# Output scatters without an order among themselves, each behind a one-element write on GpSimd

## The chip, the cores and the metric

The kernel runs on one core of one Trainium2 chip. The metric is device time in microseconds (us), the median of several runs. The engines are named as the profile names them: PE (TensorE matmuls) and PEld (its weight loads), DVE (VectorE), ACT (ScalarE), POOL (GpSimd), SP (SyncE, which only issues transfers here).

## The reference

Causal attention is followed by a mixture of experts with a capacity, and that by a dense layer pair. Cut to what matters:

```python
attn_out = attention(q, k, v, s)              # (4, 8, 576, 64), float32
x = attn_out.transpose(0, 2, 1, 3).reshape(2304, 512)
# every token goes to one of 8 experts, at most 288 tokens each, best logits first
for e in range(8):
    mask = assigned == e                       # 288 tokens
    h = np.maximum(x[mask] @ w1[e], 0.0)       # (288, 512) @ (512, 1024)
    out[mask] = h @ w2[e]
h = out @ w_in                                 # (2304, 512) @ (512, 2048)
g = np.maximum(h, 0.0) + alpha * np.minimum(h, 0.0)
return g @ w_out                               # (2304, 512)
```

The expert of a token decides the order in which the kernel works on it, and each of the 2304 output rows belongs to exactly one expert's list of 288.

## The kernel before

Attention comes first (until about 285 us of the profiled span) and leaves its result token by token in a tensor in device memory, `xd`. Then the experts are taken one after another, in the order in which a router (class `Router`) finds them. For each expert n the kernel does four things. It gathers the 288 token rows from `xd` in three blocks of 96 rows, through tiles called `stg` (`gather`, L775, an indirect DMA that GpSimd issues). It runs the expert's own two layers (`L1` and `L2` with `kind` 0). It runs the dense pair (`L1` and `L2` with `kind` 1). Last, it takes the result `oT`, which lies with features on partitions, back to token rows and scatters them to the output `out_dram`.

Every product is made of three matmuls of split operands, a high part and a low part. GpSimd makes the low parts of many of them: of the weights, `w0r` and `w1r` (L654, in `split`), and of the activations between the dense layers, `hh` (L746). So GpSimd's queue holds these subtractions and, in a fixed place among them, the gathers and scatters.

The order is written out by hand: the program's order is each engine's order, and `hook()` is called between the pieces of the matmul stream to emit the next pieces of the side tasks (`prep`, `routing`, `outs`). The scatters are such side pieces. There are 24 of them, three for each of eight experts:

- For the first seven experts `ot_dma` is used. For block j it packs 96 token columns as two-byte halves (`A`, L823 and L824), transposes them by a DMA from ScalarE's queue (`T`), puts the halves together into a `stg` tile on VectorE (`Y`, L830) and scatters that tile (`Z`, L831). `stg` has two buffers, which the gathers share: the third block of an expert uses the first block's buffer again, and the two gathers that follow use the second's and the third's. `relay` spreads the steps over the ticks; a split of a weight lies between one scatter and the next on GpSimd.
- For the eighth expert `ot` is used, at the very end: a transpose on PE, a copy on ScalarE (L787) and the scatter (L788), three times. The third block has a tile of another ring (`a64`), so none of the three waits for a buffer of the others.

A framework places the waits. It knows the scatters only as writes to the tensor `out_dram` at rows that it can't see, so each scatter waits until the one before has landed.

Of the kernel before, what the change touches and what calls it, by code (L numbers as in the profile page):

```python
# [12 lines left out]
F = dt.float32  # L13
# [24 lines left out]
TP1=0  # L38
# shifts of events against their tick and their place in it
SH={"T_peq": -0.2, "load_qk1q0": -1.58, "lg_pe": 1.83, "v3_act0_0": 0.33, "lt_act": 0.1, "load_v15": -0.27, "v2_pool": 0.06, "load_v12": 0.14, "v1_act0_0": -1.29, "spin": 0.17, "load_v11": 0.75, "T_pek": -0.1, "finish_tail": -0.2, "T_dveq": -0.13, "T_dvek_0": -0.17, "T_pek_0": -0.74, "load_qk1q2": -1.13, "v1_act1_0": -0.36, "mins20": 0.07, "T_actk_0": 0.07, "rd_4": 2.79, "lg_dve": 1.56, "load_bias": 0.68, "load_qk1q3": -0.45, "load_qk1q1": -1.43, "v2_dve_0": -0.2, "lt_pe": 1.31, "load_v14": 1.48, "load_qk1q4": -0.5, "load_qk1k1": -0.26, "v3_act1": -0.94, "T_peq_0": -4.8, "rd_1": -0.73, "load_qk1k3": -0.09, "mins00": 0.07, "tail_act": -0.1, "T_dveq_0": -0.69, "load_qk1k2": 0.42, "rd_2": -0.13, "tail_pe_0": -1.05, "tail_dve_0": -0.27, "v3_act0": 0.03, "v1_pool": 0.13, "etr2": 0.79, "v1_act0": 0.76, "rd_3": 1.2, "mins30": -0.26, "finish": 0.07, "lt_dve": 0.94, "v1_act3_0": -0.1, "av1": 1.9, "v3_dve1_0": -0.13, "v2_pool_0": 0.13, "lt_T": -0.2, "av2": 0.43, "load_v10": -0.06, "load_qk1k0": -0.32, "tail_act_0": -0.93, "v1_pool_0": -0.13, "v1_act1": 0.24, "T_actk": -0.12, "etr0": 0.23, "T_actq": 0.06, "norm_main": 0.37, "v3_dve0": 1.63, "v3_dve1": 0.11, "mins31": -0.14, "T_dvek": -0.17, "av0": 1.59, "v1_act2_0": -0.51, "etr3": 0.23, "split_lo0": 0.07, "split_lo1": 0.6, "split_hi2": -0.23, "split_lo2": -0.13, "split_hi3": 0.63, "split_lo3": 0.77}  # L40
V1N=4
ORDER=('pe0','pe1','pe2','pe3','dve0','dveA','dveB','act1','sp','dve2','act2','dve3','pl','act3','ld')
def attention(tc, q, k, v, s, w_gate, xd, L, C, cp, ap, psum, dp, hook=None, rawp=None):
    rawp=rawp or ap
    nc=tc.nc
    B,NH,S,D=4,8,576,64
    NP=B*NH//2
    idf,idb,ones=C['idf'],C['idb'],C['ones']
    # ---- loads
    warmt=ap.tile([128,8],F,name='warmt')  # L50
# [24 lines left out]
    for nm in 'qk': load_qk1(0,nm,4)  # L75
    # ---- masks
    SB=[ap.tile([128,2304],R,name=f'sb{i}') for i in range(2)]
# [5 lines left out]
    nc.vector.tensor_copy(mkt[0:64,:],mk[0:64,0:64]); nc.vector.tensor_copy(mkt[64:128,:],mk[64:128,64:128])  # L83
    # ---- keeps the array's clock up until the products begin
    def spin(n):
        tp=psum.tile([128,512],F,name='tp',bufs=TPB)
        for _ in range(n): nc.tensor.matmul(tp[:,0:128],mk,mk,start=True,stop=True)
    spin(SP0)
    # ---- cumulative sums
    nc.vector.tensor_scalar(st,st,0.0,None,op0=OP.max)  # L90
# [38 lines left out]
    for pp in range(2):  # L129
        for ab in range(2):  # L130
            # rows (pp,d) of block j: pair 2j+pp, head 2*pair+ab
            src=w_gate.rearrange("(j pp ab d) e -> pp ab d j e",j=2,pp=2,ab=2,d=64)
            nc.sync.dma_start(wgt[pp*64:pp*64+64,:,ab,:], src[pp,ab])
    ZT=ap.tile([128,2,2,128],F,name='zt'); nc.gpsimd.memset(ZT,0.0)
    # ---- q, k transposes and splits
    OPS={}
# [76 lines left out]
    def v3_dve(hb,z):  # L213
# [3 lines left out]
        nc.vector.scalar_tensor_tensor(vhl[:,1],vr,c,vhl[:,0],op0=OP.mult,op1=OP.subtract)  # L217
    # ---- scores and softmax
    SM={}; DEN={}
    # steps of a head pair: q tiles (0, 1), 2, 3 and the 64-row tail of both heads  # L220
    PARTS={0:((0,0),(1,128)),1:((2,0),),2:((3,0),)}
    WID={0:384,1:384,2:512}
    def qk(p,i):
# [3 lines left out]
        if i<3:  # L227
            qh,ql=OPS['q',p]
            # the two heads' products lie on different rows of the array and run side by side
            for ti,off in PARTS[i]:  # L230
# [163 lines left out]
    def lt_dve(b):  # L394
        r=slice(64*(b%2),64*(b%2)+64)
        nc.vector.tensor_copy(L[r,16+b//2,:],LG.pop(('l',b,4))[r,0:8])
    # ---- pipeline
    steps=[(p,i) for p in range(NP) for i in range(4)]
    n=len(steps)
# [61 lines left out]
    for t in range(tmin,tmax+1):  # L461
        while ev and ev[0][0]<t+1:
            _,f,a=ev.pop(0); f(*a)
# [3 lines left out]
NT,NE,CAP=18,8,288  # L467
# [27 lines left out]
class Router:  # L495
# [11 lines left out]
    def big(self): return self.rp.tile([128,NT*((1<<max(BS))-1)],BF,name='A')  # L507
    # The threshold t: the largest value that some open expert has CAP tokens at or above,
    # and the first such expert. Thresholds are float bits in value order, found from the top bits down.
    def search(self,mm,idx,ts,es,k):  # L510
# [5 lines left out]
        for s in range(32-B,-B,-B):  # L516
# [23 lines left out]
            if top:  # L540
                V.tensor_reduce(dig,ps[:,0:8],axis=AX.X,op=OP.max)
                # key to bits: flip the sign bit of the upper half, every bit of the lower half
                f=rp.tile([128,2],I,name='wsg')
# [18 lines left out]
    def phase(self,k,out):  # L562
# [11 lines left out]
        yield YE  # L574
        if k==NE-1: es=idx[:,0:1]; nw=NT   # one expert is left, for all the tokens left
        else:
            ts=rp.tile([128,1],F,name='ts'); es=rp.tile([128,1],F,name='es'); nw=2*NT
            for y in self.search(mm,idx,ts,es,k): yield y
# [13 lines left out]
        nc.tensor.matmul(p2[:,0:nw],self.tri,Gf,start=True,stop=True)  # L592
        # places: of the tokens above the threshold, then of those at it; 1023 and more for the others
        sc=rp.tile([128,nw],F,name='sc'); s18=rp.tile([128,NT],I,name='s18')
# [25 lines left out]
        out['idx']=idt  # L620
        # state for the next phase
        if k<NE-1:
# [11 lines left out]
class FFN:  # L634
# [11 lines left out]
    def start(self,router,xd,w1,w2,out,fp,psum):  # L646
        nc=self.nc; self.r=router; self.xd=xd; self.w1=w1; self.w2=w2; self.out=out
        self.fp=self.fpa=fp; self.psum=psum; self.idf=router.idf
        self.xT=[fp.tile([128,4,CAP],R,name=f'xT{z}') for z in 'hl']
        for c in range(self.nl,2*ND-NLOAD): self.load64(c)  # L650
    # ---- resident weights
    def split(self,h,l,x,lo_eng):
        self.nc.scalar.activation(h,x,AF.Copy)  # L653
        lo_eng.tensor_sub(l,x,h.bitcast(F))  # L654
    # float64 bits -> float32: sign and top exponent bit, seven exponent bits and 23 of the significand's.
    # Chunk 2f: w_in's columns of f-tile f; chunk 2f+1: w_out's rows. The split weights take the bits' place.
    # Where chunk c lies: a ring of its own, a slot that attention has done with, or a ring of the FFN's pool.
    def slot64(self,c,shape,dtype):
# [39 lines left out]
    def early_conv(self,n):  # L698
        for _ in range(n):
            if self.nc64<self.nl: self.cstep(1)  # L700
    # ---- expert weights
    def reg(self,n,ei):
# [10 lines left out]
    def wsplit(self,n,i):  # L713
# [4 lines left out]
        self.W[n,f,which]=w  # L718
    # ---- layers
    def L1(self,n,kind,f):  # L720
# [27 lines left out]
    def L2(self,n,kind,f):  # L748
# [12 lines left out]
        if f==last:  # L761
# [3 lines left out]
            for d in range(4):  # L765
# [4 lines left out]
                else: nc.scalar.activation(self.oT[:,d],a,AF.Copy)  # L770
    # ---- token-major ends
    def mi(self): return self.r.mi()
# [10 lines left out]
    def ot(self,idt,j,eng=None):  # L783
        nc=self.nc; ps=self.mi(); s=slice(96*j,96*j+96)
        for d in range(4): nc.tensor.transpose(ps[0:96,128*d:128*d+128],self.oT[:,d,s],self.idf)
        t=(self.fp.tile([128,512],I,name='a64',bufs=PB).bitcast(F) if j==2 else self.fp.tile([128,DM],F,name='stg',bufs=2))[0:96]
        nc.scalar.activation(t,ps[0:96,:],AF.Copy)  # L787
        nc.gpsimd.indirect_dma_start(out=self.out,out_offset=bass.IndirectOffsetOnAxis(ap=idt[:,j:j+1],axis=0),in_=t,in_offset=None)  # L788
    # the same by DMA: the transpose takes two-byte elements, so the floats go as planes of halves
    def planes(self): return self.fp.tile([128,512],I,name='a64',bufs=PB).bitcast(U16)  # L790
# [28 lines left out]
    def ot_dma(self,oT,idt):  # L819
        nc=self.nc; V=nc.vector; a={}; b={}; t={}  # L820
        def A(j):
            a[j]=self.planes(); av=a[j].rearrange("p (z d n) -> p z d n",z=2,d=4)
            V.memset(av[:,:,:,96:128],0)  # L823
            V.tensor_copy(av[:,:,:,0:96],oT.bitcast(U16)[:,:,192*j:192*j+192].rearrange("p d (n z) -> p z d n",z=2))  # L824
        def T(j):
            b[j]=self.planes()
            self.flip(b[j],a[j])
        def Y(j):
            t[j]=self.fp.tile([128,DM],F,name='stg',bufs=2)[0:96]
            V.tensor_copy(t[j].bitcast(U16).rearrange("p (e z) -> p z e",z=2),b[j][0:96].rearrange("p (z e) -> p z e",z=2))  # L830
        def Z(j): nc.gpsimd.indirect_dma_start(out=self.out,out_offset=bass.IndirectOffsetOnAxis(ap=idt[:,j:j+1],axis=0),in_=t[j],in_offset=None)  # L831
        return self.relay(A,T,Y,Z,OW)
    # ---- schedule
    def hook(self):
# [13 lines left out]
    def prep(self,n,o):  # L848
        yield lambda: self.l2done>=n   # the expert before has read its tokens and its weights
        self.reg(n,o['e'])  # L850
# [30 lines left out]
    def run(self):  # L881
# [15 lines left out]
        self.cstep(NX)  # L897
        # keeps the array's clock up while the tokens arrive
        def spin(n):
# [158 lines left out]
```

## Time and profile before

| | |
|---|---|
| median of three runs | 1031.24 us |
| the three runs | 1024.48, 1031.24, 1032.9 us |
| span of the profiled execution, first to last instruction | 1021.2 us |
| the profiled execution's own time | not given; the median lies 10.0 us above the span |
| PE busy | 913.3 us, 89% of the span |
| VectorE busy | 647.7 us, 63% |
| GpSimd busy | 501.1 us, 49% |
| ScalarE busy | 456.9 us, 45% |
| the last instruction of PE's products starts at | about 1008 us |

The span is that of one execution, taken by the hardware profiler. All rows further on are of that execution, in us from the start of the span. Issuing a transfer, a wait on a semaphore and a drain are work of an engine's queue and are not counted as busy, except that GpSimd's indirect DMAs are shown as instructions of POOL: their duration is the time in which GpSimd makes the transfer, not the transfer itself.

### The profile page before, as it was taken

What the parts mean: (1) busy time and instruction counts of PE and PEld (TensorE: products, weight loads), DVE (VectorE), ACT (ScalarE), POOL (GpSimd) and SP (SyncE); (2) the same over time, 40 slices, a digit from 0 to 9 for tenths busy, and PEclk for the clock granted to TensorE, in tenths of its full rate; (3) what the DMA queues carried; (4) which work ended last, traced back from release to release, by engine and by line L of the source; (5) the groups of instructions that cost most, each with busy time, mean ns of one, the idle gap of its engine ahead of it and who ended that gap; (6) DMA issues with size and microseconds to landing.
All of it is one profiled execution on the core that took longest, in us unless ns stands there. A gap on an engine that the chain in (4) does not pass through costs nothing.

```text
span 1021.2 us, 21290 instructions
## 1 busy us (share of the span) xinstructions
PE 913.3 (89%) x8043; PEld 844.5 (83%) x8043; DVE 647.7 (63%) x1413; ACT 456.9 (45%) x1234; POOL 501.1 (49%) x460
## 2 busy tenths in 40 slices
PE   6898999884438898999999999999999999999995
PEld 5677777763427788999999999999999999999994
DVE  7888888898885987856676545645654533332310
ACT  4677777753213334433334344334434444444332
POOL 6555655556244457725255355526526526535322
PEclk9899999986558999999999999999999999999998
DMA  6999999987765021313263035207205313422200
GB/s 124 210 240 212 212 223 211 260 182 130 237 224 180 16 64 52 98 36 98 61 158 84 17 73 143 52 22 173 67 8 137 102 29 88 127 53 73 45 1 24
DMA packets 269878, 116.10 MB, mean 114 GB/s; under 512 B 207504, under 2 KB 257040, under 8 KB 269776
## 3 DMA queue, kind: packets, MB, share of 16 engines
q1 hardware_dynamic: 127728, 70.56, 25.9%
q10 hardware_dynamic: 138976, 34.75, 20.0%
q0 software_dynamic: 3072, 9.44, 3.1%
q8 instruction: 63, 1.03, 0.4%
q14 instruction: 39, 0.32, 0.1%
HBM read 70.39 MB, written 9.58 MB: 78 GB/s over the span
## 4 chain that ended last, share of the span: by engine, by line
PE 49%; DVE 14%; DMA 6%; issue 6%; POOL 4%; ACT 2%; SPq 1%; POOLq 0%; DVEq 0%; ACTq 0%
PE hp L728 8%; PE acc L758 8%; PE hp L729 8%; PE hp L730 7%; PE acc L760 7%; PE acc L759 7%; DMA out_dram<-stg,idt 3%; PE mi L533 2%; DVE g L740 1%; POOL hh L746 1%; DMA et<-eh 1%; DVE a L680 1%; DVE a L682 1%; DVE a L681 1%; DMA rB<-in_moe_w_out_dram 1%
## 5 line engine op out<-in xcount | busy, mean ns | idle before, releaser
L746 POOL TENSOR_TENSOR hh<-g,hh 128x288 fp32r<-128x288 f32 x128 | 118.3, 925 | 246.3 <-ACT hh L745 214.9
L740 DVE SCALAR_TENSOR_TENSOR g<-g,nal 128x288 f32<-128x288 f32 x128 | 76.6, 599 | 162.2 <-ACT g L739 150.5
L294 POOL TENSOR_TENSOR eh<-e,eh 128x768 f16<-128x768 f32 (+1 forms) x48 | 91.1, 1899 | 69.7 <-DVE eh L283 43.3
L654 POOL TENSOR_TENSOR w0r<-wraw,w0r 128x512 fp32r<-128x512 f32 x62 | 89.6, 1445 | 58.2 <-ACT w0r L653 58.0
L738 ACT ACTIVATE g<-hp 128x288 f32<-128x288 f32 x128 | 52.3, 409 | 135.9 <-PE hp L730 121.8
L745 ACT ACTIVATE hh<-g 128x288 fp32r<-128x288 f32 x128 | 56.9, 444 | 117.9 <-DVE g L740 117.9
L758 PE MATMUL acc<-hh,rB 128*128 128x288 f32 x352 | 106.2, 302 | 0.0
L760 PE MATMUL acc<-hh,rB 128*128 128x288 f32 x352 | 104.3, 296 | 0.0
L759 PE MATMUL acc<-hh,rB 128*128 128x288 f32 x352 | 104.1, 296 | 0.0
L728 PE MATMUL hp<-x2h,rB 128*128 128x288 f32 x320 | 90.8, 305 | 0.0
L729 PE MATMUL hp<-x2h,rB 128*128 128x288 f32 x320 | 89.7, 300 | 0.5 <-POOL rB L654 0.5
L734 DVE SCALAR_TENSOR_TENSOR hh<-hp,hh 128x288 fp32r<-128x288 f32 x64 | 29.0, 453 | 84.7 <-ACT hh L733 84.7
L271 ACT ACTIVATE e<-sc,mn 128x128 f32<-128x128 f32 (+3 forms) x128 | 66.2, 528 | 34.5 <-DVE mn L261 24.7
L759 PE MATMUL acc<-hh,w1r 128*128 128x288 f32 x256 | 76.5, 299 | 0.9 <-POOL w1r L654 0.9
L758 PE MATMUL acc<-hh,w1r 128*128 128x288 f32 x256 | 77.1, 301 | 0.0
L760 PE MATMUL acc<-hh,w1r 128*128 128x288 f32 x256 | 76.1, 297 | 0.0
L728 PE MATMUL hp<-xTh,w0r 128*128 128x288 f32 x256 | 73.9, 308 | 0.9 <-ACT xTh L781 0.6
L729 PE MATMUL hp<-xTh,w0r 128*128 128x288 f32 x256 | 73.2, 305 | 0.3 <-POOL w0r L654 0.3
L758 PEld LDWEIGHTS acc<-hh,rB 128*128 128x128 f32 x352 | 66.5, 189 | 0.3
L760 PEld LDWEIGHTS acc<-hh,rB 128*128 128x128 f32 x352 | 66.5, 189 | 0.0
L654 POOL TENSOR_TENSOR w1r<-wraw,w1r 128x512 fp32r<-128x512 f32 x46 | 64.1, 1393 | 4.8 <-ACT w1r L653 4.6
L759 PEld LDWEIGHTS acc<-hh,rB 128*128 128x128 f32 x352 | 66.3, 188 | 0.0
(297 smaller groups left out, 2907.6 us busy)
## 6 DMA issues: line engine op xcount, KB each, us to landing
wraw<-in_moe_w_dram SPq DMA_DIRECT2D x128, 256.0 KB
rB<-in_moe_w_out_dram SPq DMA_DIRECT2D x11, 512.0 KB
rB<-in_moe_w_in_dram SPq DMA_DIRECT2D x10, 512.0 KB
qr<-in_q_dram SPq DMA_DIRECT2D x32, 128.0 KB
kr<-in_k_dram SPq DMA_DIRECT2D x32, 128.0 KB
vr<-in_v_dram SPq DMA_DIRECT2D x32, 128.0 KB
xd<-xm SPq DMA_DIRECT2D x16, 256.0 KB
rA<-in_moe_w_in_dram SPq DMA_DIRECT2D x3, 512.0 KB
```

What stands on the lines that cost most here:

```text
L271: nc.scalar.activation(e[:,h,off:off+N],sc[:,off:off+N],AF.Exp,bias=mn[:,2*z+h:2*z+h+1],scale=-1.0,accum_out=den[:,2*ti+h:2*ti+h+1])
L294: nc.gpsimd.tensor_sub(e4[:,:,1],e[:,:,:N],e4[:,:,0])
L654: lo_eng.tensor_sub(l,x,h.bitcast(F))
L728: nc.tensor.matmul(ps,wh[k],x[0][:,k],start=(k==0),stop=False)
L729: nc.tensor.matmul(ps,wl[k],x[0][:,k],start=False,stop=False)
L730: for k in range(4): nc.tensor.matmul(ps,wh[k],x[1][:,k],start=False,stop=(k==3))
L740: nc.vector.scalar_tensor_tensor(g,g2[:,1],self.nal[:,f:f+1],g,op0=OP.mult,op1=OP.add)
L745: nc.scalar.activation(hh[:,0],g,AF.Copy)
L746: nc.gpsimd.tensor_sub(hh[:,1],g,hh[:,0].bitcast(F))
L758: nc.tensor.matmul(a,wh[:,ds],hh[:,0],start=(f==0),stop=False)
L759: nc.tensor.matmul(a,wl[:,ds],hh[:,0],start=False,stop=False)
L760: nc.tensor.matmul(a,wh[:,ds],hh[:,1],start=False,stop=(f==last))
```

## The change

The two places that issue a scatter call a new function. It writes one element of a new tile `mark` on GpSimd and then issues the scatter, which is put into a group whose members are declared to have no dependence on each other. Waits of a scatter for its data, and of others for a scatter, are not touched by the declaration. Nothing reads `mark`. (The diff also takes out comments.)

```diff
@@ start
         self.xT=[fp.tile([128,4,CAP],R,name=f'xT{z}') for z in 'hl']
+        self.mark=fp.tile([1,1],F,name='mark')
@@ ot
-        nc.gpsimd.indirect_dma_start(out=self.out,out_offset=bass.IndirectOffsetOnAxis(ap=idt[:,j:j+1],axis=0),in_=t,in_offset=None)
+        self.scatter(idt,j,t)
+
+    def scatter(self,idt,j,t):
+        self.nc.gpsimd.memset(self.mark,0.0)
+        i=self.nc.gpsimd.indirect_dma_start(out=self.out,out_offset=bass.IndirectOffsetOnAxis(ap=idt[:,j:j+1],axis=0),in_=t,in_offset=None)
+        self.tc.declare_no_dep(i.ins,group='out',reason='rows of different tokens')
+        self.tc.add_to_no_dep_group('out',i.ins)
@@ ot_dma
-        def Z(j): nc.gpsimd.indirect_dma_start(out=self.out,out_offset=bass.IndirectOffsetOnAxis(ap=idt[:,j:j+1],axis=0),in_=t[j],in_offset=None)
+        def Z(j): self.scatter(idt,j,t[j])
```

## Rows read from the trace of the kernel before

**Rows 1.** The page's head, and busy time in two stretches of the span.
```profile
span 1021.2 us, 21290 instructions
...
600.00:700.00 100.00, 98.51 (x810) 95.54 (x809) 51.95 (x123) 41.30 (x96) 53.09 (x45) 1.00 0.37 85
...
1000.00:1021.00 21.00, 8.53 (x63) 7.70 (x61) 0.69 (x2) 4.88 (x11) 4.37 (x5) 0.79 0.10 28
```

**Rows 2.** PE's waits from 320 us to the end: total us, times, longest.
```profile
PE mi L613 <- DVE rb L609: 5.7, 4, 2.0
...
PE acc L760 <- POOL hh L746: 2.2, 2, 1.2
...
PE acc L759 <- POOL w1r L654: 0.9, 3, 0.5
```

**Rows 3.** GpSimd's instructions by line: count, busy us, mean ns, idle before.
```profile
L831 POOL DMA_INDIRECT out_dram<-stg,idt x21 | 20.3, 965 | 36.9 <-DMA out_dram<-stg,idt 19.7 <-DVE stg L830 4.3 <-DVE hh L734 4.0
```

**Rows 4.** GpSimd's timeline around the third expert's scatters: start, us, idle before.
```profile
612.06 0.94 POOL L831 DMA_INDIRECT out_dram<-stg,idt  x1 [0.15 <-issue]
...
616.87 0.93 POOL L831 DMA_INDIRECT out_dram<-stg,idt  x1 [2.54 <-DMA out_dram<-stg,idt]
617.82 1.29 POOL L654 TENSOR_TENSOR w1r<-wraw,w1r 128x512 fp32r<-128x512 f32 x1
621.83 0.92 POOL L831 DMA_INDIRECT out_dram<-stg,idt  x1 [2.71 <-DMA out_dram<-stg,idt]
...
625.74 1.95 POOL L775 DMA_INDIRECT stg<-xd,idt  x1 [1.74 <-PE hp L730]
627.72 1.55 POOL L746 TENSOR_TENSOR hh<-g,hh 128x288 fp32r<-128x288 f32 x2
```

**Rows 5.** VectorE's timeline in the same stretch.
```profile
614.80 0.75 DVE L830 COPY stg<-a 96x1024 uint16<-96x1024 uint16 x1
...
619.07 0.76 DVE L830 COPY stg<-a 96x1024 uint16<-96x1024 uint16 x1 [0.86 <-DMA a<-a]
```

**Rows 6.** The timeline of the last 13 us, ScalarE's last copy and GpSimd.
```profile
1008.44 0.92 POOL L788 DMA_INDIRECT out_dram<-stg,idt  x1 [3.69 <-ACT stg L787]
1008.90 0.59 ACT L787 ACTIVATE a<-mi 96x512 f32<-96x512 f32 x1 [0.25 <-PE mi L785]
1011.98 0.92 POOL L788 DMA_INDIRECT out_dram<-stg,idt  x1 [2.62 <-DMA out_dram<-stg,idt]
1015.51 0.92 POOL L788 DMA_INDIRECT out_dram<-a,idt  x1 [2.61 <-DMA out_dram<-stg,idt]
```

**Rows 7.** The chain that ended last, its last stretch: start, us, what.
```profile
1008.44 2.76 DMA out_dram<-stg,idt
...
1011.24 0.74 issue
```

**Rows 8.** GpSimd's timeline, first gathers after attention: indirect DMAs issued back to back.
```profile
299.07 1.15 POOL L775 DMA_INDIRECT stg<-xd,idt  x1 [3.12 <-DVE acc L624]
300.52 1.36 POOL L775 DMA_INDIRECT stg<-xd,idt  x1 [0.31 <-issue]
```

**Rows 9.** Small writes of GpSimd at the start of the program, by line.
```profile
L1040 POOL MEMSET const-float32-1.0<- 128x1 f32 x1 | 0.1, 107 | 0.0
```

**Rows 10.** The program's last line: GpSimd's drains, ns min/median/max, first and last start.
```profile
L1054 POOLq DRAIN  x3: 40/102/5133, 1015.3 to 1021.0; - x3
```

**Rows 11.** Busy time in 1008.4 to 1012.0 us; DMA share and GB/s last.
```profile
1008.40:1012.00 3.60, 0.46 (x4) 0.21 (x2) 0.00 (x0) 0.84 (x2) 0.94 (x2) 1.00 0.20 57
```

**Rows 12.** A scatter of the first expert and VectorE's copy beside it.
```profile
431.60 1.30 POOL L831 DMA_INDIRECT out_dram<-stg,idt  x1 [0.16 <-issue]
...
431.59 0.49 DVE L824 COPY a<-x2h 128x768 uint16<-128x768 uint16 x1
```

**Rows 13.** Busy time in 523 to 528 us; granted clock third from the end.
```profile
523.00:528.00 5.00, 4.76 (x38) 4.73 (x38) 4.73 (x15) 0.63 (x1) 2.49 (x2) 0.66 0.54 147
```

**Rows 14.** Time from issue to landing of the first three gathers, 295 to 330 us.
```profile
DMA to landing us min/median/max: 3.7/6.8/8.3
```

## The prediction

> **What bounds the kernel now.** I read the page's head first, then busy time by stretches. From about 500 us on the kernel is a stream of matmuls: between 600 and 700 us PE is busy 98.5 of 100 us at a granted clock of 1.00, GpSimd 53 [rows 1]. Nothing that GpSimd does can count there unless PE waits for it. The last 21 us are different: PE is busy 8.5 of them [rows 1], its work is over at about 1008 us, and what follows is a chain with one step at a time.
>
> Next I read who PE waits for from 320 us on. Two groups name GpSimd: 2.2 us in two waits for `hh`, 0.9 us in three waits for `w1r`, together 3.1 us [rows 2]. The dearest single cause is another: 5.7 us in four waits of the router's product for `rb` on VectorE, the longest 2.0 us [rows 2].
>
> Then I read the scatters. 21 of the 24 have line 831; GpSimd sat idle 36.9 us before them, 19.7 of it until an earlier scatter had landed [rows 3]. The other three stand at the end of the program, and there the wait before the second and the third is 2.62 and 2.61 us [rows 6]. So the order among scatters costs GpSimd some 25 us of idle time. The question is how much of it lies on the path that sets the end.
>
> **The change part by part.** *The last three scatters.* They start at 1008.44, 1011.98 and 1015.51 us, 3.54 and 3.53 us apart [rows 6]. Such a step is the landing, 2.76 us from the issue, and 0.74 us more until the next one is under way [rows 7], with a few hundredths for the wait. Their data are no obstacle: the third block's copy starts at 1008.90 and takes 0.59 us, so it is done at 1009.49, and the second block's was done before it [rows 6]. Without the order, a step is what GpSimd itself needs: 0.92 us for the scatter [rows 6], about 0.10 for the small write (107 ns for a 128x1 write [rows 9]; no 1x1 write is in the trace, and a smaller one is hardly dearer), and the gap in front of an indirect DMA behind another, 0.31 us [rows 8]. That is 1.33 us. The third scatter then starts at 1008.44 + 2.66 = 1011.10 in place of 1015.51: 4.4 us earlier. The first write costs nothing, since GpSimd idles 3.69 us before the first scatter [rows 6]. Bounds on the step: 0.92 + 0.15 = 1.07 us, if only the short gap of a scatter behind a subtraction applies [rows 4] and the write hides in it, and 1.36 + 0.31 + 0.10 = 1.77 us by the slower of the two gathers [rows 8]. The gain lies between 3.5 and 4.9 us.
>
> What comes after the last scatter could eat this. GpSimd's final drain takes 5.13 us from 1015.3 [rows 10], so it ends at 1020.4, while the scatter that it follows should have landed at 1015.51 + 2.76 = 1018.3: 2.2 us more. With one scatter open the surplus is 2.2 us; with three open the trace has no row. If each open scatter added such a surplus in turn, 4.4 us would be added and the gain would be nil; it may as well not grow at all. I take no growth, because the drain starts with a single scatter in flight in the only row there is and I see nothing that would make it go by scatters. So the tail is worth 4.4 us, with ends 0 and 4.9.
>
> *The transfers in the tail.* The DMA engines are busy 0.20 of the 3.6 us around the first scatter [rows 11], 0.7 us of all sixteen for one scatter. That is below the step of 1.33 us, so one is through before the next arrives, and I keep the landing time at 2.76 us. The far end is the three gathers issued back to back, which took 3.7 to 8.3 us to land [rows 14], but beside heavy loads that the tail doesn't have.
>
> *The 21 scatters in the middle.* Take the third expert's [rows 4]. The second scatter waits 2.54 us for the first; its data, a copy that starts at 614.80 and takes 0.75 us, are there at 615.55 [rows 5], so it can go at about 615.75, 1.1 us earlier than 616.87. The split of `w1r` behind it moves with it, and PE's wait for that goes. The third scatter's data come at 619.07 + 0.76 = 619.83 [rows 5], so it goes at about 620.05 in place of 621.83, 1.8 us earlier; from here the data, not the order, are late. Behind it stand two gathers that write into `stg` buffers still being read by the second and third scatter. They keep their waits: the wait moves from the third scatter to the first gather, and the second gather still waits for the third scatter's landing. That landing is 1.8 us earlier, so `hh`, at 627.72 now, comes up to 1.8 us earlier. This is one of the two `hh` waits of 1.0 and 1.2 us (2.2 in all), and both should go. The other stands behind the sixth expert's scatters, and the three `w1r` waits behind the third, the sixth and the seventh expert's. Behind the other four groups PE names nothing of GpSimd, so an earlier start is worth nothing there. I take the whole 3.1 us of [rows 2] as the gain; the bounds are 0 (VectorE becomes late in the same places) and 3.1 plus one vanished router stall.
>
> *The small write.* 21 x 0.1 us = 2.1 us of GpSimd time in the middle. It waits for nothing, so it runs at once behind the instruction ahead of it, where GpSimd sits idle for want of data or room. If that cover is gone in all 24 places, it costs 2.4 us.
>
> *A rule against it.* A scatter that starts beside VectorE's copy at 431.59 took 1.30 us in place of 0.93 or so [rows 4, 12], 0.37 us more. The Trainium skill, page "SBUF — State Buffer", section "SBUF: two separate sides", warns that GpSimd cannot write a DMA's descriptors while VectorE runs a two-port operation such as a float32 copy. The trace agrees in kind, 1.30 against 0.93 us. By the rule each moved scatter could be held for the length of such a copy, and the sum of the middle would be smaller; by the row it keeps its gain. Here the moved scatters follow the copy that makes their data, by about 0.2 us, and at most 0.37 us of the 1.1 to 1.8 would be lost. In the tail VectorE does nothing [rows 11].
>
> Sum: 4.4 + 3.1 = 7.5 us. The profiled execution's own time isn't given; its span, 1021.2 us [rows 1], lies 10.0 us below the median of 1031.24, and nothing of the change touches what lies outside. So the span should be 1013.7 us and the median 1031.24 - 7.5 = 1023.7 us.
>
> **Rivals.** *Tail only: 1026.8 us.* The PE waits in the middle are replaced by others: `hh` also needs ScalarE's and VectorE's work, and a gather behind the third scatter keeps its wait for the landing. For it: the wait moves rather than goes. Against: PE's named waits there end on GpSimd. 1031.24 - 4.4 = 1026.8.
>
> *More than counted: 1020.0 us.* GpSimd's earlier work clears VectorE's router chain of one stall. Each has a price: 2.0 us of wait [rows 2], and in the 5 us after such a stall the granted clock averaged 0.66 [rows 13], a part of it at 1.2 in place of 2.4 GHz, which is 5 x 0.34 = 1.7 us: 3.7 in all. One stall less gives 1020.0, two 1016.3.
>
> *Open scatters get in each other's way: 1029.7 us.* If a scatter doesn't move before the earlier one has landed, only the 0.74 us and the wait itself, 0.78 us, are saved twice, and the middle gains nothing: 1031.24 - 1.6. Against it is the low DMA share.
>
> *The change doesn't do what it says: 1031 to 1034 us.* If the waits stay, for the buffers or for a reason of the framework's, the 24 writes are all that is new, from 0 to 2.4 us. Against: in the tail the three tiles are different, so only the order can hold them.
>
> *Slower: 1038.5 us.* GpSimd's subtractions move by 1 to 2 us against VectorE's router chain, and where they now fall beside its long operations both take longer (a gather took 1.95 us at 625.74, against 0.92 for the scatters [rows 4]). If the router's product becomes late by a stall of 3.7 us in a further phase, half the gain is gone; from the third such phase on (3 x 3.7 = 11.1 against 7.5) the kernel is slower, and with four it is at 1031.24 - 7.5 + 14.8 = 1038.5. Over 1% slower takes five of the six phases behind a group. Against: the chain has few such stalls now, four in 700 us.
>
> **How the numbers follow.** Chances: forecast 0.42, tail only 0.27, more than counted 0.13, scatters in each other's way 0.05, no effect 0.07, slower 0.06. The range reaches from 1018, which takes in the case of one stall less and part of that of two, to 1031, which takes in the 1029.7 and the drain's bound without the middle; beyond it lie slower, most of no effect and part of the low case, about 2 in 10. A measurement of this kernel can tell about 1% from no change, 10.3 us: the three runs alone span 8.4 us. 1% faster is below 1020.9. That holds most of the case of one stall less or more, and some of the forecast's own spread by the runs: 0.25. Slower by over 1%, above 1041.6, takes the slower case at its worst: 0.04. The rest is 0.71.
>
> **What would show it.** Right: the last three scatters some 1.3 us apart with no wait between them, the span's end some 5.7 us behind the third as now (1021.2 - 1015.51), no wait of a line-831 scatter for `out_dram`, gathers that now carry the wait for a landing, and no `hh` or `w1r` wait of PE around 615 to 630, 865 to 885 and 945 to 955 us. Wrong: a drain well above 5.1 us, a landing well above 2.8 us in the tail, or new waits of PE for the router's VectorE steps. What would make the number wrong with every step right is a shift of the whole stream in its first 400 us, where no scatter stands.

## The result, and the profile after

| | before | after |
|---|---|---|
| median, first comparison (4 runs each) | 1032.07 us | 1018.58 us |
| ratio, first comparison | | 0.9882, 95% interval 0.9836 to 0.9927 |
| ratio, second comparison (9 runs against 28) | | 0.9908, 95% interval 0.9873 to 0.9943 |
| span of the profiled execution | 1021.2 us | 1017.2 us |
| that execution's own time | | 1019.14 us |

The change makes the kernel faster, by about 1%. (A ratio is estimated from all runs of its comparison and isn't the quotient of the two medians.) The two ratios make 12.2 us (7.5 to 16.9) of 1032.07 and 9.5 us (5.9 to 13.1) of 1028.62. The spans differ by 4.0 us only. The reason is that the profiled execution of before had a short attention stage: its first gather starts at 299.07 us [rows 8], that of after at 305.79. The next section shows how far such starts scatter.

The end of the kernel first. GpSimd's timeline over the last 10 us, after; it answers to [rows 6] and [rows 9]:

```profile
1009.01 0.92 POOL L793 DMA_INDIRECT out_dram<-stg,idt  x1 [3.66 <-ACT stg L788]
1009.93 0.09 POOL L792 MEMSET mark<- 1x1 f32 x1
1010.24 0.92 POOL L793 DMA_INDIRECT out_dram<-stg,idt  x1 [0.22 <-ACT a L788]
1011.16 0.09 POOL L792 MEMSET mark<- 1x1 f32 x1
1011.46 0.92 POOL L793 DMA_INDIRECT out_dram<-a,idt  x1 [0.22 <-issue]
```

The scatters are 1.23 us apart where they were 3.54: 0.92 for the scatter, 0.09 for the write, 0.22 until the next is under way. The third starts 2.45 us behind the first, before 7.07.

The program's last line after, GpSimd's drains (ns min/median/max, first and last start); it answers to [rows 10]:

```profile
L1061 POOLq DRAIN  x3: 40/102/6272, 1010.1 to 1016.9; - x3
```

The long drain is 1.14 us longer than before, but it also starts earlier against the last scatter: just ahead of the second scatter (1010.1 against 1010.24), where before it started just ahead of the third (1015.3 against 1015.51). It ends at 1016.4, 4.9 us after the start of the third scatter, as before (1020.4 against 1015.51). The end of the span is 5.71 us behind the start of the last scatter in both executions, so the drain doesn't grow with three scatters open. Nor does the landing: in a second execution of the changed kernel (`both_again` below) each of the last three scatters took 2.7 us from issue to landing, against 2.7 to 2.8 us before.

The middle, by the third expert's scatters again. GpSimd's timeline after; it answers to [rows 4]:

```profile
618.74 0.94 POOL L793 DMA_INDIRECT out_dram<-stg,idt  x1 [0.16 <-issue]
...
622.52 0.93 POOL L793 DMA_INDIRECT out_dram<-stg,idt  x1 [1.49 <-DVE stg L837]
623.47 1.30 POOL L655 TENSOR_TENSOR w1r<-wraw,w1r 128x512 fp32r<-128x512 f32 x1
624.70 0.09 POOL L792 MEMSET mark<- 1x1 f32 x1
625.77 0.92 POOL L793 DMA_INDIRECT out_dram<-stg,idt  x1 [0.98 <-DVE stg L837]
...
631.42 0.99 POOL L776 DMA_INDIRECT stg<-xd,idt  x1 [3.48 <-DMA out_dram<-stg,idt]
632.43 1.31 POOL L747 TENSOR_TENSOR hh<-g,hh 128x288 fp32r<-128x288 f32 x1
```

From the first scatter to the second are 3.78 us (before 4.81), to the third 7.03 (before 9.77), and to `hh` 13.69 (before 15.66). The second and third scatter wait for VectorE's copy of their data now. The second gather waits 3.48 us for the third scatter's landing: the wait has moved down the queue.

GpSimd's waits from 330 us to the end, after (total us, times, longest):

```profile
POOL out_dram L793 <- DVE stg L837: 21.5, 13, 3.0
POOL stg L776 <- DMA out_dram<-stg,idt: 11.1, 5, 3.5
```

No scatter waits for a scatter any more, where 19.7 [rows 3] and 5.2 us [rows 6] were so spent. But the wait for data has grown from 4.3 us [rows 3] to 21.5, and the gathers' wait for a landing from 2.1 us to 11.1. GpSimd, busy 501.9 us of the span where it was 501.1, is hardly less idle; it is only idle at other points.

PE's waits from 320 us to the end, after; these rows answer to [rows 2]:

```profile
PE mi L613 <- DVE rb L609: 5.0, 4, 1.6
...
PE acc L761 <- POOL hh L747: 0.9, 1, 0.9
```

Of the 3.1 us that named `hh` and `w1r` before, 0.9 us is left, and that stands at a new place, near 548 us; at the three places that the prediction named nothing is left. The router's stalls are still there, 5.0 us against 5.7.

### The profile page after: what moved, and what is told of

Same layout as the page of the kernel before. It is cut to its first block, busy times and chain, and to the rows that moved or that the text cites. A ratio compares the mean times of both kernels' runs of the same rounds, so it can differ in the third digit from the quotient of the medians.

```text
span 1017.2 us, 21304 instructions
## 1 busy us (share of the span) xinstructions
PE 914.2 (90%) x8043; PEld 845.3 (83%) x8043; DVE 647.6 (64%) x1413; ACT 456.6 (45%) x1234; POOL 501.9 (49%) x484
## 4 chain that ended last, share of the span: by engine, by line
PE 54%; DVE 13%; DMA 4%; issue 4%; ACT 2%; POOL 2%; SPq 1%; ACTq 0%; POOLq 0%; DVEq 0%
PE hp L729 9%; PE acc L759 8%; PE hp L731 8%; PE hp L730 8%; PE acc L761 8%; PE acc L760 8%; PE mi L533 2%; DMA et<-eh 1%; DVE a L683 1%; DVE g L741 1%; DVE a L682 1%; DVE a L681 1%; DMA rB<-in_moe_w_out_dram 1%; DMA x2h<-xd,idt 1%; SPq L670 1%
## 5 line engine op out<-in xcount | busy, mean ns | idle before, releaser
L746 ACT ACTIVATE hh<-g 128x288 fp32r<-128x288 f32 x128 | 56.9, 444 | 118.2 <-DVE g L741 115.5
L729 PE MATMUL hp<-xTh,w0r 128*128 128x288 f32 x256 | 71.9, 303 | 0.8 <-ACT xTh L782 0.6
L730 PE MATMUL hp<-xTh,w0r 128*128 128x288 f32 x256 | 70.6, 297 | 0.7 <-POOL w0r L655 0.7
```

The lines of the kernel that those rows point to most:

```text
L729: nc.tensor.matmul(ps,wh[k],x[0][:,k],start=(k==0),stop=False)
L730: nc.tensor.matmul(ps,wl[k],x[0][:,k],start=False,stop=False)
L746: nc.scalar.activation(hh[:,0],g,AF.Copy)
```

## The experiments

Two theories stood at the outset. A: both parts of the change count, the tail with 4.6 us and the middle with 3 to 7. B: only the tail counts, and the middle's gain in the first two traces is chance.

To compare executions I use marks that every trace has: the start of the first of the 128 copies `hh<-g` on ScalarE (L745 before, L746 after), the start of ScalarE's last copy `a<-mi`, and the end of the span. The first is about 79 us ahead of the first scatter, the second falls into the tail. The rows of before for the first mark, by line (last column: first and last start), and of after:

```profile
L745 ACT ACTIVATE hh<-g x128: 442/444/447, 352.7 to 1003.4; 128x288 fp32r<-128x288 f32 x128
```

```profile
L746 ACT ACTIVATE hh<-g x128: 442/444/447, 359.4 to 1004.0; 128x288 fp32r<-128x288 f32 x128
```

In all twelve profiled executions (us; the middle is the second mark less the first, the tail is the span less the second mark). "Low clock" is the time within the middle in which the granted clock of PE was at its lower level, 1.2 in place of 2.4 GHz, added up from the trace's clock records. "Waits" is how long PE's weight loads (PEld) waited for GpSimd between 420 and 1005 us:

| kernel | first mark | middle | tail | span | own time | low clock | waits |
|---|---|---|---|---|---|---|---|
| before | 352.7 | 656.2 | 12.3 | 1021.2 | | 10.2 | 4.9 |
| before_again | 360.4 | 657.7 | 12.3 | 1030.4 | 1032.18 | 9.4 | 6.1 |
| tail_only | 357.2 | 655.2 | 7.7 | 1020.2 | 1021.95 | 12.8 | 2.4 |
| write_only | 360.1 | 654.5 | 12.5 | 1027.1 | 1028.89 | 6.8 | 4.6 |
| after | 359.4 | 650.1 | 7.7 | 1017.2 | 1019.14 | 3.4 | 1.6 |
| both_again | 359.5 | 651.7 | 7.7 | 1018.8 | 1020.80 | 6.8 | 1.0 |
| middle_only | 361.5 | 652.0 | 12.2 | 1025.7 | 1027.74 | 9.5 | 0.8 |
| write_in_tail | 359.4 | 650.0 | 7.7 | 1017.2 | 1018.97 | 6.8 | 0.8 |
| three_buffers | 357.7 | 652.4 | 8.2 | 1018.3 | 1020.05 | 9.4 | 0.8 |
| nine_writes | 356.5 | 659.9 | 9.9 | 1026.4 | 1028.16 | 15.7 | 7.1 |
| nine_first_two | 359.4 | 656.2 | 7.7 | 1023.4 | 1025.17 | 10.2 | 6.0 |
| nine_third | 364.1 | 652.9 | 7.7 | 1024.7 | 1026.44 | 6.8 | 2.5 |

Two things are read from it at once. The first mark scatters by 11 us from execution to execution, with no regard to the kernel, and it lies where no scatter has been issued yet: of the 9.2 us between the spans of before and before_again, one and the same kernel, 7.7 lie ahead of it, and the first trace of before was the earliest of all. And an execution's own time is its span plus 1.7 to 2.0 us.

The expectations quoted below give the tail of before as 14.4 us: they count from ScalarE's last copy `x2h<-acc`, which stands 2.1 us ahead of the second mark. So their tails are 2.1 us longer than the table's and their middles 2.1 us shorter.

**both_again**: the changed kernel once more.

> The changed kernel once more, for a second execution and a closer interval. Theory A (both parts count): about 11 us under the kernel before, ratio near 0.989; in the trace the tail from the last product to the end is 4.6 us shorter, and from the first expert to the last product another 3 to 7 us are gone. Theory B (only the tail counts, the middle's gain in the first pair of traces is chance): about 4.5 us, ratio 0.9956.

Ratio 0.9908 (0.9873 to 0.9943), 9.5 us. Middle 651.7 and tail 7.7 us, close to the first trace's. Theory A's figure was 11, B's 4.5; the interval leaves B out.

**tail_only** and **middle_only**: one part each.

```diff
 tail_only, in ot_dma:
-        def Z(j): self.scatter(idt,j,t[j])
+        def Z(j): nc.gpsimd.indirect_dma_start(out=self.out,...,in_=t[j],in_offset=None)
 middle_only, in ot:
-        self.scatter(idt,j,t)
+        nc.gpsimd.indirect_dma_start(out=self.out,...,in_=t,in_offset=None)
```

> Only the last expert's three scatters are without an order; the 21 in the middle wait for each other as before. Theory A: 4.5 us under the kernel before (ratio 0.9956), less than half of the whole gain. Theory B: the same 4.5 us, and no different from the kernel with both parts.

> Only the 21 scatters in the middle are without an order; the last three wait for each other as before. Theory A: 3 to 7 us under the kernel before (ratio 0.993 to 0.997), the tail as long as before (start of the last scatter 7.1 us behind the first). Theory B: no change, ratio 1.000.

tail_only: ratio 0.9938 (0.9903 to 0.9973), 6.4 us; tail 7.7, middle 655.2. middle_only: ratio 0.9948 (0.9923 to 0.9973), 5.3 us; tail 12.2, middle 652.0. Each part alone is faster than before, and within the intervals the two make up the whole. Theory B falls with middle_only. By its time alone that would be thin, since write_only below came out 3.4 us under before in the same comparison; the marks carry it, 652.0 us for the middle where the kernels with the order have 654.5 to 657.7. The waits of PE's weight loads on GpSimd between 420 and 1005 us show what the middle part takes away. First before, then tail_only, then after:

```profile
PEld acc L760 <- POOL hh L746: 3.3, 4, 1.4
...
PEld acc L759 <- POOL w1r L654: 1.6, 3, 0.7
```

```profile
PEld acc L760 <- POOL w1r L655: 1.6, 2, 1.2
...
PEld acc L761 <- POOL hh L747: 0.8, 3, 0.3
```

```profile
PEld acc L761 <- POOL hh L747: 1.6, 3, 1.2
```

Read so, before loses 4.9 us to GpSimd in the middle, where PE's own waits name 3.1. A weight load stands ahead of its matmul, and a wait that both rows show is 0.23 or 0.24 us longer for the load. `w1r` makes 1.6 to 2.0 us in each of the four executions with the order (in write_only under another name, see there) and is gone from all five without it. `hh` varies more, from 0.8 to 4.5 us with the order and from 0.8 to 1.6 without. Tail_only, order and all, lost only 2.4 us to GpSimd.

**write_only**: the writes, with the order kept (the two lines that declare no dependence are left out).

> The 24 small writes are there, and every scatter still waits for the one before. Both theories: 0 to 2.4 us over the kernel before; in the tail the write runs before the wait for the landing ends and costs nothing. If the small write itself does good (it parts the scatter from the instruction ahead of it), this kernel would be faster than before.

Ratio 0.9967 (0.9937 to 0.9997): 3.4 us under before where 0 to 2.4 over had been expected, by an interval that just misses no change. The traces don't bear out a gain: the tail is 12.5 us, no shorter, the middle 654.5, and GpSimd still holds up the weight loads:

```profile
PEld acc L761 <- POOL hh L747: 2.6, 3, 1.2
PEld acc L760 <- POOL mark L792: 2.0, 4, 0.7
```

(`mark` stands here for the split of `w1r`: the wait ends with the split, and the write right behind it, for the next scatter, ends within 0.02 us of it.) So I take it for chance. Write_in_tail supports that, since the middle loses nothing without the writes; before_again, 0.7 us off, says little either way.

**before_again**: before against itself.

> The kernel before against itself. Ratio 1.000 within its interval. If the 3.4 us by which the kernel with writes alone came out below the kernel before is chance, this one may come out as far off. In its trace: the tail from the last copy 14.4 us as before, from the first expert's gathers to the last copy 650 to 655 us, and a granted clock at its lower level for 3.4 us near 810 us, as in all three kernels with the order kept in the middle.

Ratio 1.0007 (0.9978 to 1.0037); tail 12.3, middle 657.7, or 655.5 as the expectation counts. The expected stretch of low clock near 810 us is not there (the granted clock is 1.00 from 800 to 825 us), a miss.

**write_in_tail**: no order, and no write ahead of the 21.

```diff
-    def scatter(self,idt,j,t):
-        self.nc.gpsimd.memset(self.mark,0.0)
+    def scatter(self,idt,j,t,write=True):
+        if write: self.nc.gpsimd.memset(self.mark,0.0)
...
-        def Z(j): self.scatter(idt,j,t[j])
+        def Z(j): self.scatter(idt,j,t[j],False)
```

> No scatter waits for another, and the small write stands ahead of the last three scatters alone; the 21 in the middle have none. If the writes do nothing but take GpSimd's time where it idles, this is the changed kernel: ratio 0.990, tail 9.7 us, middle 647 to 649 us. If the write itself helps in the middle, it loses up to 3 us against the changed kernel.

Ratio 0.9900 (0.9874 to 0.9927), middle 650.0, tail 7.7: the changed kernel's figures. A write of 0.09 us ahead of each middle scatter can't be seen, neither as a help nor as a cost. A kernel without the writes in the tail was not run.

**three_buffers**: the changed kernel with three `stg` buffers (`bufs=2` to `bufs=3`, four places).

> The changed kernel with three buffers in place of two for the tile that scatters read and gathers write. The second gather then waits for the second scatter's landing, not the third's, so the wait that moved from scatters to gathers (11.1 us in 5 waits) shrinks below 5 us. If that moved wait still holds PE, the middle is 1 to 3 us shorter than 647 to 649 us; if not, it stays there. I expect it to stay, ratio 0.990.

Ratio 0.9903 (0.9880 to 0.9926), middle 652.4, or 650.3 as the expectation counts, 1.3 us above its range. The moved wait is all but gone, 0.3 us against 11.1 in the row above (waits of GpSimd from 330 us on, three_buffers):

```profile
POOL stg L776 <- DMA out_dram<-stg,idt: 0.3, 1, 0.3
```

The time stays, and the middle is no shorter, so the gathers' wait costs nothing that can be seen where it stands now.

**nine_writes**: eight more writes ahead of each of the 24 scatters.

```diff
-        self.nc.gpsimd.memset(self.mark,0.0)
+        for _ in range(9): self.nc.gpsimd.memset(self.mark,0.0)
```

> Nine small writes ahead of each scatter in place of one. Each took 0.09 us in the changed kernel. In the middle they run where GpSimd idles and cost nothing; in the tail eight more stand between the scatters twice, so the third scatter starts 0.5 to 1.5 us later against the first (2.45 us in the changed kernel). Time 1 us over the changed kernel, ratio 0.991. If the writes were a cost in the middle, it would show eightfold: up to 17 us.

Ratio 0.9973 (0.9941 to 1.0005): most of the gain is given back. The median is 8.4 us above that of write_in_tail in the same comparison. GpSimd's timeline in the tail:

```profile
1015.98 0.92 POOL L793 DMA_INDIRECT out_dram<-stg,idt  x1 [2.48 <-ACT stg L788]
1016.90 1.26 POOL L792 MEMSET mark<- 1x1 f32 x9
1018.32 0.92 POOL L793 DMA_INDIRECT out_dram<-stg,idt  x1 [0.16 <-issue]
1019.24 1.26 POOL L792 MEMSET mark<- 1x1 f32 x9
1020.66 0.92 POOL L793 DMA_INDIRECT out_dram<-a,idt  x1 [0.16 <-issue]
```

Nine writes take 1.26 us, 1.17 more than one. In the tail the steps are 2.34 us in place of 1.23, twice, and the tail grew by just that, 2.2 us. The middle was the miss. I had expected the writes to be hidden there, and it went to 659.9 us, 8.7 over the mean of the five kernels without an order (651.2). A part of that is the clock: 15.7 us of this middle were at the lower level, 7.2 in the mean of the five. Half of the time at the lower level is what it costs at most, so as an estimate 4.2 of the 8.7 us are the clock's and 4.5 are left. The medians lie between, 8.4 us less the 2.2 of the tail, 6.2. GpSimd does have idle time around the scatters, and the writes use it up (its wait for data ahead of them shrinks from 21.5 to 1.8 us), but the work behind a scatter comes later all the same.

**nine_first_two** and **nine_third**: the nine writes only ahead of some of the middle's scatters, one in the tail.

```diff
 both:
-    def scatter(self,idt,j,t):
-        self.nc.gpsimd.memset(self.mark,0.0)
+    def scatter(self,idt,j,t,n=1):
+        for _ in range(n): self.nc.gpsimd.memset(self.mark,0.0)
...
 nine_first_two:
-        def Z(j): self.scatter(idt,j,t[j])
+        def Z(j): self.scatter(idt,j,t[j],9 if j<2 else 1)
 nine_third:
-        def Z(j): self.scatter(idt,j,t[j])
+        def Z(j): self.scatter(idt,j,t[j],9 if j==2 else 1)
```

> No order among the scatters; in the middle nine small writes ahead of each expert's first and second scatter, behind which a weight's split stands on GpSimd, and one ahead of the third; in the tail one each. Theory C (the middle's gain comes from the splits of weights): most of the 7 to 8 us that nine writes everywhere cost in the middle comes back here, middle near 653 us, ratio near 0.995. Theory D (it comes from the activations' subtraction behind the third scatter and the gathers): little, middle 648 to 650 us, ratio 0.991.

> The same with nine writes ahead of each expert's third scatter alone, behind which the two gathers and the first subtraction for the dense layers stand. Theory C: middle 648 to 650 us, ratio 0.991. Theory D: middle near 653 us, ratio near 0.995.

nine_first_two: ratio 0.9935 (0.9894 to 0.9976), middle 656.2, 5.0 us over the mean. nine_third: ratio 0.9867 (0.9830 to 0.9904), middle 652.9, 1.7 us over. At equal clock, by the same estimate, it is 3.5 and 1.8 us. Theory C fits best: GpSimd's lateness costs most where a weight's split stands behind it. But it is one trace each, the 1.7 us are less than the 2.4 by which the five themselves differ, and the ratio of nine_third shows no cost at all. PEld's waits on GpSimd from 420 to 1005 us in nine_first_two, and then in nine_third:

```profile
PEld hp L730 <- POOL mark L792: 2.6, 5, 0.5
...
PEld acc L760 <- POOL mark L792: 1.8, 5, 0.4
PEld acc L761 <- POOL hh L747: 1.6, 3, 1.2
```

```profile
PEld acc L761 <- POOL hh L747: 2.5, 3, 1.2
```

Two lines fall on the splits, once per expert for five experts (`mark` again for the split that ends just ahead of it). But the order that the change removes delayed other things than these writes do: it never delayed the split behind the first scatter, and before lost more at `hh` (3.3 us) than at `w1r` (1.6). Nor is the 2.5 us of nine_third the writes' lateness alone: two gathers that met an operation of VectorE's make 2.3 of it (see "The rule against it" below).

## Why the prediction was right, and where its sizes were off

*The tail.* Right, step by step. Forecast 4.4 us from a step of 1.33; measured 4.6 from a step of 1.23. The mean tail of the four kernels with the order kept there is 12.3 us (before, before_again, write_only, middle_only), of those without it and with one write 7.7 (8.2 with three buffers). The gap ahead of a scatter is 0.22 us with the write in between, not the 0.31 of two gathers back to back. The drain, whose growth was the lower bound, doesn't grow: last scatter to end is 5.71 us in ten of the traces, 5.72 in write_in_tail and 6.16 in three_buffers.

*The middle.* The place was right, the term was too small: 3.1 us forecast. The middle's mean is 655.9 us for the four kernels with the order kept there (656.2, 657.7, 655.2, 654.5) and 651.2 for the five without it (650.1, 651.7, 652.0, 650.0, 652.4), 4.7 us apart, with no overlap. The term that was mis-sized is the sum of PE's waits that name GpSimd. PEld's waits are the fuller account: 4.5 us in the mean of the four, 1.0 in that of the five, 3.5 less. (The prediction passed over a third group of PE's waits that names GpSimd, 0.5 us for `rB`; it stands ahead of the first scatter, before and after, out of the change's reach.)

*The rest of the middle.* It is about the size of a difference in the clock. The four middles with the order hold 9.8 us at the lower level in the mean, the five without it 7.2. Taking off half of the time at the lower level, which is an estimate, leaves 651.0 and 647.6 us, about 3.4 apart, close to the 3.5 of PEld's waits. Tail_only, which waited least of the four, then has 648.8 us, the others 651.0 to 653.0.

Whether the change has a hand in the clock is not settled. One stretch looks like it, in the windows from 800 to 825 us, before and then after (granted clock third from the end):

```profile
800.00:825.00 25.00, 22.98 (x176) 22.81 (x175) 13.34 (x25) 10.26 (x26) 12.68 (x13) 0.93 0.27 67
```

```profile
800.00:825.00 25.00, 23.53 (x191) 23.29 (x191) 14.48 (x31) 11.14 (x29) 13.30 (x14) 1.00 0.30 84
```

The 25 us at 0.93 in place of 1.00 lose 1.75 by the clock, and 15 matmuls fewer, at 23.53/191 us each, are 1.8 us, of which the stall ahead of the dip, 0.5 us longer before, has a part. This dip stands in three of four executions with the order in the middle and in none of five without. But before_again has the order without the dip, nine_writes and nine_third have the dip without the order, and that stall, 1.5 to 2.0 us for the router's `rb`, is there in all twelve. What decides over the dip was not found. The 2.0 us of vanished stall that the rival "more than counted" reckoned with didn't come.

*The wait that moved to the gathers.* Right: 11.1 us of it, and taking it away changed nothing (three_buffers).

*The small write.* Its price, about 0.1 us, was right (0.09). That it runs where GpSimd is idle is only in part the reason. It holds ahead of an expert's second and third scatter, which mostly wait for their data (13 waits of 21 scatters); ahead of the first, GpSimd goes straight on, and the split behind it comes later. Nine writes, 1.17 us more ahead of 21 scatters, cost 8.7 us in the middle, 4.5 at equal clock: 0.18 to 0.35 us of the kernel's time for each us of GpSimd's. At that share 21 single writes cost 0.3 to 0.7 us, too little to be seen here.

*The rule against it.* The prediction priced VectorE's hold on GpSimd at 0.37 us for a scatter. For scatters that was about right: the median took 0.933 us before and after, and the few long ones (up to 1.30 us before, 1.41 after) ran beside a copy, a split or a router operation of VectorE's. For the gathers behind them it was too little. Before, the third expert's second gather starts at 625.74, while VectorE runs an operation of the router:

```profile
625.55 1.33 DVE L523 TENSOR_TENSOR A<-mm,ci 128x1134 bf16<-128x1134 f32 x1
```

That gather took 1.95 us [rows 4], and the weight loads then waited 1.25 us for the `hh` behind it. From 400 us on, the twelve traces have 14 indirect DMAs that start while this operation runs, ten of them second gathers. Every one ended 0.80 or 0.81 us after the operation did; the ten gathers took 1.44 to 2.10 us, where an undisturbed one takes 0.93, and behind each of the ten stands a wait of 1.15 to 1.25 us for `hh`. This agrees with the rule of the Trainium skill, page "SBUF — State Buffer", section "SBUF: two separate sides", that VectorE can lock GpSimd out of writing a DMA's descriptors; whether this operation is of the kind that the page names, no row shows. So the `hh` part of the prediction had the place right and half of the reason: `hh` was late not only for the order, but also where the gather ahead of it fell on VectorE's operation. Such gathers number four in the four executions with the order in the middle, one in the five without (after, at 545.42 us, which is its remaining `hh` wait) and five in the three with nine writes. They make about 1.0 of the 3.5 us by which PEld's waits differ. Whether the change avoids them or only happened to was not tested.

*The rivals.* Tail only is refuted by middle_only, scatters in each other's way by the unchanged 5.71 us and the 1.23 us steps, no effect and slower by the result. More than counted has the number nearest to the first comparison, 1020.0 us, but not its mechanism: no stall went.

*The sum.* 4.6 + 4.7 = 9.3 us against 7.5, and the second comparison's 9.5. The first comparison's 12.2 has 9.3 well within its interval; the absolute 1018.58 us was below the forecast of 1023.7 because both the gain and the luck of the runs were larger. It lies only 0.6 us above the range's lower end, 1018, and in the case of over 1% faster, which had been given 0.25; the second comparison's nine runs had a median of 1020.55. The working also held that the span lies 10.0 us below the time. That was wrong: it is 1.7 to 2.0 us, and the trace of before was simply of a short execution (first mark 352.7 us, the others 356.5 to 364.1). The forecast span, 1013.7, failed for that: 1017.2 came, the 4.0 us between the spans being 6.1 from the middle and 4.6 from the tail less 6.6 by which the first mark was later.

## What to carry to other kernels

An order among writes to one output buys nothing where they go to different rows, and it costs a landing for each write at the end of a program, where nothing hides it; there 2 x 2.3 us came back. In the middle of a stream look at what stands behind the waiting instruction on its queue, and count the weight loads' waits beside the matmuls': an engine that is busy half of the time can still be late just there. An indirect DMA that GpSimd starts while VectorE runs a long operation may be held until that is over, so look where a moved gather lands. Compare traces by marks within them, since one stage that varies by 11 us hides a gain of 9.

## What the runs showed that I had not expected

GpSimd, 49% busy, has less slack around the scatters than that suggests: 1.17 us more ahead of each of 21 cost 8.7 us in one trace, about half of it by the clock. Most came from the 14 scatters with a weight's split behind them (5.0 us, 3.5 at equal clock); the 1.7 of the other 7 are not clear of the spread between executions. A gather that starts beside VectorE's operation of 1.33 us takes up to 2.10 us in place of 0.93. The first 350 us vary by 11 us between executions of the same or of nearly the same program, with no scatter in them. And the program's end is 5.71 us behind the start of the last scatter in ten of twelve traces, with one scatter open or three: 2.7 us until it lands, about 2.2 us more in which GpSimd's drain goes on, and the rest until the last instruction.
